# Block sums of the weights in smaller pieces over both halves of two batches, VectorE's part as scalar_tensor_tensor, the last token products three units sooner

## The chip, the cores and the metric

The kernel runs on one core of one Trainium2 chip. The metric is device microseconds of one execution (lower is better). The engines are named as in the profile: PE is TensorE (PEld its weight loads), DVE is VectorE, ACT is ScalarE, POOL is GpSimd, SP is SyncE, which here issues nearly all DMAs. Each engine takes its instructions in the order in which they were written for it.

## The reference

Attention with a local window and 24 block summaries per head, and then a mixer over tokens and over channels, for 4 batches of 768 tokens and 8 heads of 64:

```
k_sum, v_sum = max and mean of k, v over blocks of 32 tokens
scores = [local (|i-j| < 16) , q k_sum + log 32] / 8 ;  x = softmax(scores) @ [v, v_sum]
u  = x + (relu(x^T w_tok1) w_tok2)^T        # w_tok1 768x256, w_tok2 256x768
out = u + relu(u w_ch1) w_ch2               # w_ch1 512x1536, w_ch2 1536x512
```

## The kernel before

Matrix products run in a reduced fp32 form (fp32r): each operand is split into a high part (a copy on ACT) and the rest (a subtraction on DVE or POOL), and three of the four part products are summed. The work is written into a list by hand; a planner (`Plan._order`) with a cost and a rank for each item simulates the engines and fixes the order of the instructions of each engine. A lower rank goes first; the block sums have the last one (`R_BACK`).

Per batch b = 0..2 the channel mixer runs in 24 units called slots: 12 for the first 512 tokens (half 0) and 12 for the last 256 (half 1). In each, `ch1` multiplies u by one of 12 column blocks of w_ch1 (tile `hp`), ACT and DVE make the two parts of relu (tile `h`), and `ch2` adds h times a block of w_ch2 to the sums (`acc`); `ch1` of the next slot is written ahead of `ch2` of this one. Beside these slots stands the attention of batch b+1 (scores `sc`, products with v `av` that give `x`), and near their end the token products of batch b+1: `tok1x` makes high and low parts of x (`xs`) and of w_tok1 (`ws`), the low parts on POOL, 12 for a batch, and sums products into `t1q`; `tok2` multiplies its relu `t` by w_tok2 into `up` and makes `u`. `finish` adds u to `acc` on DVE and POOL (`ot`) and stores it.

Batch 3 goes another way: `last_mix` replaces eight block products of 2x2 blocks by seven (in two rounds, w_ch1 and w_ch2). It needs sums and differences of u's blocks (`t_2`, `t_3`, `t1`, `t4`, shown as `t`, from the scratch tiles `t32` and `t33`) and, for each of 6 row pairs k of both weights, four sums of weight blocks (s1 to s4). These twelve sets are made ahead by `weight_sums(w, k, tag)`: subtractions on POOL and DVE into `sz`, the high part on ACT into `sh`, the rest on POOL in place, then two DMAs of 512 KB to DRAM (`sums`), from which `last_mix` loads them. In the kernel before, each of batches 0 to 2 makes four sets, in slots 13, 14, 15 and 17, in buffers of the tags `u0` and `h`, which other tiles use too (`u0` holds u, `xs` and `ws`).

Of the kernel before, what the change touches and what calls it, by code (L numbers as in the profile page):

```python
# [189 lines left out]
def tile_attention_mixer(  # L190
# [574 lines left out]
    def tok2(b, half, p):  # L765
# [37 lines left out]
        if far:  # L803
# [9 lines left out]
            if whole and half and p < 2:  # L813
# [9 lines left out]
                lambda: (nc.vector, nc.gpsimd)[half].tensor_tensor(  # L823
                    out=u.t[:, 1], in0=xT(), in1=u.t[:, 0].bitcast(F32), op=ALU.subtract
                ),
# [144 lines left out]

    def weight_sums(w, k, tag):

        blk, keys = blocks(w, k)
# [6 lines left out]
        def step(eng, s, left, right, op):  # L980
            e = nc.gpsimd if eng == "pool" else nc.vector
            add(
                eng, 0.8 if eng == "pool" else 0.34,
                lambda: e.tensor_tensor(out=z.t[:, s], in0=left(), in1=right(), op=op),  # L984
                reads=keys, writes=[(z, s)], rank=R_BACK, behind=gate,
            )
# [17 lines left out]
        step("dve", 3, part("12", 0), own(1), ALU.subtract)
        step("dve", 3, own(3), part("12", 1), ALU.add)
        for ss in ((0, 1), (2, 3)):
            cs = slice(ss[0], ss[1] + 1)
# [5 lines left out]
            add(
                "pool", 1.1,
                lambda cs=cs: nc.gpsimd.tensor_tensor(  # L1015
                    out=z.t[:, cs].bitcast(F32R), in0=z.t[:, cs], in1=hi.t[:, cs].bitcast(F32),
                    op=ALU.subtract,
                ),
                reads=[(hi, ss)], writes=[(z, s) for s in ss], rank=R_BACK,
            )  # L1020
        add(
            "sp", 0.06, lambda: nc.sync.dma_start(out=away.t[:, 0], in_=hi.t.bitcast(F32)),
            reads=[(hi, ss) for ss in ((0, 1), (2, 3))], writes=[(away, 0)], kb=524,
        )
        add(
            "sp", 0.06, lambda: nc.sync.dma_start(out=away.t[:, 1], in_=z.t),
            reads=[(z, s) for s in range(4)], writes=[(away, 1)], kb=524,
        )
# [617 lines left out]
```

## Time and profile before

| | |
|---|---|
| median of 3 runs | 603.72 us (603.57 to 606.78) |
| the profiled execution | 604.11 us, its span 602.3 us |
| busy | PE 568.4, PEld 495.3, DVE 383.0, ACT 257.2, POOL 265.5 us |
| L984, subtractions of the sums | 60 on POOL; 60 on DVE, 50.0 us |
| L1015, low parts of the sums, POOL | 24, 32.8 us |
| L732, low parts of xs and ws, POOL | 36, 47.0 us |

The span is 1.8 us shorter than the execution's own time. Busy PE time counts overlapping matmuls to their modelled ends, so a stretch with no idle time may still run slower than PE could; the start of one group of matmuls to the start of the next is the better measure. In the rows, `x12` is a count of instructions, "[1.09 <-DVE h L870]" is idle time before the group and what ended it, and L984 is a line of the kernel. A helper's line stands for all its callers.

### The profile page before, as it was taken

How to read it: one execution, taken by the hardware profiler on the slowest of the kernel's cores; microseconds unless marked ns; L12 is line 12 of the kernel's file. 1: busy time of each engine (PE TensorE's matmuls, PEld its weight loads, DVE VectorE, ACT ScalarE, POOL GpSimd, SP SyncE). 2: the span in 40 equal slices, each digit the busy share in tenths (PEclk: the TensorE clock that was granted, in tenths of full speed). 3: DMA queues.
4: the chain of work that ended last, by engine and by line, in shares of the span. 5: the costliest groups of instructions: out<-in, count | busy, mean ns of one | idle time of the engine just before them, and what ended most of it. 6: DMA issues, size and time to landing. Idle time of an engine off the chain costs nothing. (4 is left out here: it accounts for less than half of the span.)

```text
span 602.3 us, 12729 instructions
## 1 busy us (share of the span) xinstructions
PE 568.4 (94%) x4629; PEld 495.3 (82%) x4629; DVE 383.0 (64%) x994; ACT 257.2 (43%) x777; POOL 265.5 (44%) x301
## 2 busy tenths in 40 slices
PE   8799999899889999999999799999998987999997
PEld 4588888778779978777889777877788976999997
DVE  4678799988993355354596255444369348435875
ACT  5577665444574342232242334242222433334542
POOL 0226586736872700000387850010059895344611
PEclk9889999999999999999999899999999998999999
DMA  8933568644776149687797654675485524578732
GB/s 276 344 115 124 187 222 264 210 140 162 257 233 209 52 141 261 177 269 196 230 233 268 172 102 133 138 186 144 97 205 159 171 104 140 194 234 266 245 106 75
DMA packets 139919, 112.12 MB, mean 186 GB/s; under 512 B 88272, under 2 KB 118608, under 8 KB 139856
## 3 DMA queue, kind: packets, MB, share of 16 engines
q1 hardware_dynamic: 139712, 111.10, 61.2%
q8 instruction: 37, 0.61, 0.4%
q14 instruction: 26, 0.21, 0.1%
q10 hardware_dynamic: 144, 0.20, 0.1%
HBM read 74.90 MB, written 34.60 MB: 182 GB/s over the span
## 5 line engine op out<-in xcount | busy, mean ns | idle before, releaser
L896 PE MATMUL acc<-h,w 128*128 128x512 f32 (+1 forms) x864 | 167.0, 342 | 4.5 <-DVE h L870 4.4
L853 PE MATMUL hp<-u,w 128*128 128x512 f32 (+1 forms) x864 | 165.5, 341 | 0.8 <-ACT u L817 0.6
L896 PEld LDWEIGHTS acc<-h,w 128*128 128x128 f32 x864 | 134.1, 189 | 25.8 <-DVE h L870 5.6
L853 PEld LDWEIGHTS hp<-u,w 128*128 128x128 f32 x864 | 134.2, 190 | 21.8 <-issue 1.3
L450 ACT ACTIVATE e<-e,den 128x120 f32<-128x120 f32 x192 | 73.3, 385 | 41.3 <-DVE den L440 35.1
L865 ACT ACTIVATE h<-hp 128x512 fp32r<-128x512 f32 (+1 forms) x72 | 35.1, 487 | 130.6 <-PE hp L853 130.4
L870 DVE SCALAR_TENSOR_TENSOR h<-hp,h 128x512 fp32r<-128x512 f32 (+1 forms) x72 | 39.6, 549 | 66.0 <-ACT h L865 66.0
L409 POOL MEMSET e<- 128x48 f32 x16 | 2.2, 138 | 129.8 <-DMA away<-e 74.3
L440 DVE CUSTOM_DVE_ANT_0 e<-sc,mask_sb 128x120 f32<-128x120 f32 x192 | 41.4, 276 | 10.9 <-PE sc L426 7.6
L790 PE MATMUL up<-wt,t 128*128 128x512 f32 (+2 forms) x192 | 42.3, 360 | 4.3 <-DVE t L685 2.7
L1460 POOL TENSOR_TENSOR w<-wb,w 128x256 fp32r<-128x256 f32 x48 | 38.0, 810 | 18.1 <-ACT w L1454 17.7
L790 PEld LDWEIGHTS up<-wt,t 128*128 128x128 f32 x192 | 32.2, 199 | 9.2 <-DVE t L685 4.4
L984 POOL TENSOR_TENSOR sz<-sz,w 128x256 f32<-128x256 f32 x48 | 37.9, 790 | 3.3
L1015 POOL TENSOR_TENSOR sz<-sz,sh 128x512 fp32r<-128x512 f32 x24 | 32.8, 1373 | 9.5 <-ACT sh L1010 4.7
L746 PE MATMUL t1q<-xs,ws 128*128 128x256 f32 x216 | 32.3, 302 | 4.7 <-POOL ws L732 3.2
L450 ACT ACTIVATION_READ_ACCUMULATOR e<-e,den 128x1 f32 x192 | 36.3, 189 | 0.0
L746 PEld LDWEIGHTS t1q<-xs,ws 128*128 128x128 f32 x216 | 29.8, 205 | 6.4 <-POOL ws L732 4.1
L984 DVE TENSOR_TENSOR sz<-sz,w 128x256 f32<-128x256 f32 x36 | 32.5, 908 | 0.8
L935 POOL TENSOR_TENSOR ot<-ot,u 128x512 f32<-128x512 f32 (+1 forms) x24 | 24.3, 1043 | 19.1 <-DVE ot L927 15.4
L426 PE MATMUL sc<-k,q 64*64 64x120 f32 x768 | 29.0, 275 | 1.9 <-PE et L488 0.7
L426 PEld LDWEIGHTS sc<-k,q 64*64 64x64 f32 x768 | 21.1, 135 | 10.8 <-issue 6.6
L557 PEld LDWEIGHTS av<-v,eT 120*64 120x64 f32 x768 | 24.0, 138 | 7.0 <-issue 4.7
(130 smaller groups left out, 899.4 us busy)
## 6 DMA issues: line engine op xcount, KB each, us to landing
w<-in_w_ch SPq DMA_DIRECT2D x48, 256.0 KB
k<-in_kw SPq DMA_DIRECT2D x16, 720.0 KB
v<-in_vw SPq DMA_DIRECT2D x32, 288.0 KB
q<-in_q SPq DMA_DIRECT2D x16, 384.0 KB
sums<-sh SPq DMA_DIRECT2D x12, 512.0 KB
...
```

Of the source, the lines that this page charges most:

```text
L426: nc.tensor.matmul(tiles[j].t[c * QT : (c + 1) * QT, i * NC : (i + 1) * NC], lhsT=qt.t[rows, t * QT : (t + 1) * QT], rhs=kt.t[rows, t, :], ...
L440: nc.vector.tensor_tensor_reduce(out=e.t[:, j, i * P : i * P + NC], in0=tiles[j].t[:, i * NC : (i + 1) * NC], in1=mask_sb[:, mv, :], op0=A ...
L450: nc.scalar.activation(ei, ei, AF.Exp, bias=den_t[n].t[:, 1, T : T + 1], scale=-1.0, accum_out=den_t[n].t[:, 0, T : T + 1],)
L746: nc.tensor.matmul(pt.t[:, 2 * P * k : 2 * P * (k + 1)], lhsT=ws[:, wp, T, ks], rhs=xs[:, xp, T], start=(c == 0 and k == 0 and T == 0 and ...
L790: nc.tensor.matmul(pt.t[:, :nt], lhsT=t1.t[:, part, ks], rhs=wt2[w].t[:, k, h0 : h0 + nt], start=(far and k == 0 and i == 0), stop=(k == D ...
L853: nc.tensor.matmul(pt.t[:, :nt], lhsT=w1_t[f].t[:, w, c], rhs=us[c].t[:, part], start=(i == 0), stop=(i == len(ops) - 1),)
L865: lambda: nc.scalar.activation(h.t[:, 0], pt.t[:, :nt], AF.Relu),
L870: lambda: nc.vector.scalar_tensor_tensor(out=h.t[:, 1], in0=pt.t[:, :nt], scalar=0.0, in1=h.t[:, 0].bitcast(F32), op0=ALU.max, op1=ALU.sub ...
L896: nc.tensor.matmul(slot.t[:, c0 : c0 + nt], lhsT=w2_t[f].t[:, w, o * P : (o + 1) * P], rhs=h.t[:, part], start=(f == 0 and w == 0 and part ...
L984: lambda: e.tensor_tensor(out=z.t[:, s], in0=left(), in1=right(), op=op),
L1015: lambda cs=cs: nc.gpsimd.tensor_tensor(out=z.t[:, cs].bitcast(F32R), in0=z.t[:, cs], in1=hi.t[:, cs].bitcast(F32), op=ALU.subtract,),
L1460: lambda hi=hi, lo=lo, source=source: nc.gpsimd.tensor_tensor(out=lo(), in0=source(), in1=hi().bitcast(F32), op=ALU.subtract),
```

## The change

`weight_sums` makes each set in two pieces. Piece 0 (s1, s2) is summed by POOL alone, 5 instructions; piece 1 (s3, s4) by DVE alone, 6 (5 before, since s4 now takes the two parts of piece 0's second sum in turn). Each piece has its own ACT copy, its own POOL remainder and two DMAs of 256 KB instead of a share of two DMAs of 512 KB. DVE's instructions there, in `last_mix`'s sums and splits, and in one split of `tok2` become `scalar_tensor_tensor` with a multiplication by 1 (`between`); the reciprocal's addition of 1e-9 becomes one too. The sets now stand in slots 14 and 17 of batch 0, and in 6, 8, 10, 13, 15 of batch 1 and 6, 8, 10, 12, 14 of batch 2; those of half 0 use the tag `t1`, the others `h`, none `u0`. For batch 3 the attention ends earlier (a1 is 26, not 29), `tok1x` stands in slots 16 and 17 (not 18 and 20), and `tok2` from slot 18 to 21 (not 20 to 22).

```diff
+    def between(eng, out_, left, right, op):
+        if eng == "pool":
+            nc.gpsimd.tensor_tensor(out=out_, in0=left, in1=right, op=op)
+        else:
+            nc.vector.scalar_tensor_tensor(
+                out=out_, in0=left, scalar=1.0, in1=right, op0=ALU.mult, op1=op
+            )
...
-                nc.vector.tensor_scalar(
-                    out=rec.t, in0=den.t[:, 0], scalar1=1e-9, scalar2=None, op0=ALU.add
+                nc.vector.scalar_tensor_tensor(
+                    out=rec.t, in0=den.t[:, 0], scalar=1e-9, in1=den.t[:, 0], op0=ALU.add,
+                    op1=ALU.max,
...
-        step("dve", 2, part("11", 0), part("21", 0), ALU.subtract)
-        step("dve", 2, own(2), part("11", 1), ALU.add)
-        step("dve", 2, own(2), part("21", 1), ALU.subtract)
...
-        step("dve", 3, part("12", 0), own(1), ALU.subtract)
-        step("dve", 3, own(3), part("12", 1), ALU.add)
...
+                step("dve", 0, part("11", 0), part("21", 0), ALU.subtract)
+                step("dve", 0, own(0), part("11", 1), ALU.add)
+                step("dve", 0, own(0), part("21", 1), ALU.subtract)
+                step("dve", 1, part("12", 0), old(1, 0), ALU.subtract)
+                step("dve", 1, own(1), old(1, 1), ALU.subtract)
+                step("dve", 1, own(1), part("12", 1), ALU.add)
...
-            for at_slot, tag in ((13, "u0"), (14, "h"), (15, "u0"), (17, "h")):
+    SUMS = ((14, 17), (6, 8, 10, 13, 15), (6, 8, 10, 12, 14))
+            if slot in SUMS[b]:
+                weight_sums(1 + n // HALF, n % HALF, "t1" if half == 0 else "h")
+        if b == B - 2:
+            a1 = 26
+            t1s = (16, 17)
-            t2s = [(20, 0, 0), (20, 0, 1), (21, 1, 0), (21, 1, 1)]
-            t2s += [(22, 1, 2), (22, 1, 3), (22, 0, 2), (22, 0, 3)]
+            t2s = [(18, 0, 0), (18, 0, 1), (19, 1, 0), (19, 1, 1)]
+            t2s += [(20, 1, 2), (20, 1, 3), (21, 0, 2), (21, 0, 3)]
```

How the engines' orders change, at three places. The first is PE at the end of batch 2's slots. `acc` ends these slots, `t1q` and `up` are batch 3's token products, `pa`, `pb`, `pc` are `last_mix`'s first products. Before:

```order
L896 MATMUL acc_1_0_5406<-h_1_10_5819,w_10_1630 128x256 x6
L896 MATMUL acc_1_2_5407<-h_1_10_5819,w_10_1630 128x256 x6
L896 MATMUL acc_1_0_5406<-h_1_11_5859,w_11_1719 128x256 x6
L896 MATMUL acc_1_2_5407<-h_1_11_5859,w_11_1719 128x256 x6
L746 MATMUL t1q_0_5775<-xs_0_1_5839,ws_0_1_5842 128x256 x12
L746 MATMUL t1q_0_5775<-xs_0_2_5856,ws_0_2_5861 128x256 x12
L790 MATMUL up_0_0_5922<-wt_0_632,t_3_0_5913 128x384
```

The same place of PE now:

```order
L895 MATMUL acc_1_0_5488<-h_1_10_6086,w_10_1630 128x256 x6
L895 MATMUL acc_1_2_5489<-h_1_10_6086,w_10_1630 128x256 x6
L895 MATMUL acc_1_0_5488<-h_1_11_6114,w_11_1719 128x256 x6
L895 MATMUL acc_1_2_5489<-h_1_11_6114,w_11_1719 128x256 x6
L1115 MATMUL pa_6134<-u_0_0_5801,w_0_885 128x384 x3
L1115 MATMUL pa_6134<-u_0_1_5816,w_0_885 128x384 x3
L1115 MATMUL pb_6146<-t_5942,s_0_5872 128x384 x6
L1115 MATMUL pc_6182<-t_6144,s_0_5955 128x384 x6
```

The five sets of `t1q` and eight `up` that stood behind the last `acc` (two sets and the first line of one `up` are shown) now all stand ahead of it, between slots 14 and 19 of 24, and `last_mix` follows `acc` at once. POOL at the same end: `ot` is batch 2's last sums, `t_6051` (now `t_6131`) is `t33`, `t_6067` (now `t_6144`) the low part of `t_3`, which `pc` reads, `t_0` and `t_1` are those of t4. Before:

```order
L935 TENSOR_TENSOR ot_1_0_5947<-ot_1_0_5947,u_1_3_4923 128x256
L1053 TENSOR_TENSOR t_6051<-u_1_1_5593,u_1_0_5321 128x384
L823 TENSOR_TENSOR u_1_2_6049<-u_1_1_5593,u_1_2_6049 128x384
L1068 TENSOR_TENSOR t_6067<-t_6051,t_6067 128x384
L1053 TENSOR_TENSOR t_6051<-u_1_1_5593,u_1_0_5321 128x384
L823 TENSOR_TENSOR u_1_3_6089<-u_1_1_5593,u_1_3_6089 128x384
L1068 TENSOR_TENSOR t_6067<-t_6051,t_6067 128x384
L1068 TENSOR_TENSOR t_0_6112<-t_6051,t_0_6112 128x384
```

POOL there now:

```order
L1040 TENSOR_TENSOR s_5_1_5891<-s_5_1_5891 128x512
L973 TENSOR_TENSOR t_6131<-u_1_1_5687,u_1_0_5400 128x384
L934 TENSOR_TENSOR ot_1_0_6129<-ot_1_0_6129,u_1_0_4651 128x256
L934 TENSOR_TENSOR ot_1_0_6129<-ot_1_0_6129,u_1_1_4761 128x256
L934 TENSOR_TENSOR ot_1_0_6129<-ot_1_0_6129,u_1_2_4910 128x256
L934 TENSOR_TENSOR ot_1_0_6129<-ot_1_0_6129,u_1_3_4915 128x256
L973 TENSOR_TENSOR t_6144<-t_6131,t_6144 128x384
L973 TENSOR_TENSOR t_6131<-u_1_1_5687,u_1_0_5400 128x384
L973 TENSOR_TENSOR t_0_6177<-t_6131,t_0_6177 128x384
L973 TENSOR_TENSOR t_6144<-t_6131,t_6144 128x384
```

The four `ot` stand between the first `t33` and its low part, so all of `t_3` now waits for `finish` of batch 2.

The second place is POOL at the end of batch 1's slots, ahead of batch 2's token products (`sz`, now `s`, are the sums; L1015, now L1040, their low parts). Before:

```order
L1015 TENSOR_TENSOR sz_0_3997<-sz_0_3997,sh_0_4090 128x512 x2
L732 TENSOR_TENSOR xs_0_0_4164<-x_0_3220,xs_0_0_4164 128x512
L732 TENSOR_TENSOR ws_0_0_4179<-wt_388,ws_0_0_4179 128x512
L984 TENSOR_TENSOR sz_1_4211<-w_1_1016,w_7_1464 128x256
L984 TENSOR_TENSOR sz_1_4211<-sz_1_4211,w_1_1016 128x256
L984 TENSOR_TENSOR sz_1_4211<-sz_1_4211,w_7_1464 128x256
L984 TENSOR_TENSOR sz_1_4211<-sz_1_4211,w_1_1016 128x256 x2
L1015 TENSOR_TENSOR sz_1_4211<-sz_1_4211,sh_1_4280 128x512 x2
L732 TENSOR_TENSOR xs_0_1_4315<-x_0_3220,xs_0_1_4315 128x512
```

POOL there now, where xs and ws 0_0 and 0_1 stand still further ahead:

```order
L733 TENSOR_TENSOR xs_0_2_4139<-x_0_3188,xs_0_2_4139 128x512
L733 TENSOR_TENSOR ws_0_2_4148<-wt_388,ws_0_2_4148 128x512
L1040 TENSOR_TENSOR s_5_1_4001<-s_5_1_4001 128x512
L973 TENSOR_TENSOR s_0_0_4143<-s_0_0_4143,w_0_929 128x256
L973 TENSOR_TENSOR s_0_0_4143<-s_0_0_4143,w_6_1383 128x256
L973 TENSOR_TENSOR s_0_0_4143<-s_0_0_4143,w_0_929 128x256 x2
L1040 TENSOR_TENSOR s_0_0_4143<-s_0_0_4143 128x512
L934 TENSOR_TENSOR ot_1_0_4322<-ot_1_0_4322,u_1_0_3010 128x256
L934 TENSOR_TENSOR ot_1_0_4322<-ot_1_0_4322,u_1_1_3141 128x256
L934 TENSOR_TENSOR ot_1_0_4322<-ot_1_0_4322,u_1_2_3252 128x256
L934 TENSOR_TENSOR ot_1_0_4322<-ot_1_0_4322,u_1_3_3341 128x256
L1040 TENSOR_TENSOR s_0_1_4308<-s_0_1_4308 128x512
```

The six instructions for the first half of x are now done ahead of the sums; behind the last row shown follow the six for the second half (xs_1, ws_1).

The third place is DVE in half 0 of batch 2, slots 8 and 9 (`h_0_8`, `h_0_9`; `rec` is the reciprocal of the attention's sums). Before:

```order
L870 SCALAR_TENSOR_TENSOR h_0_8_5129<-hp_0_8_5084,h_0_8_5129 128x512
L563 TENSOR_SCALAR rec_5137<-den_4980 128x6
L566 RECIPROCAL rec_5137<-rec_5137 128x6
L870 SCALAR_TENSOR_TENSOR h_0_9_5171<-hp_0_9_5142,h_0_9_5171 128x512
L870 SCALAR_TENSOR_TENSOR h_0_10_5204<-hp_0_10_5177,h_0_10_5204 128x512
```

DVE there now:

```order
L869 SCALAR_TENSOR_TENSOR h_0_8_5175<-hp_0_8_5132,h_0_8_5175 128x512
L975 SCALAR_TENSOR_TENSOR sl_2_1_5199<-w_2_1138 128x256
L975 SCALAR_TENSOR_TENSOR sl_2_1_5199<-sl_2_1_5199,w_2_1138 128x256 x2
L975 SCALAR_TENSOR_TENSOR sl_2_1_5199<-w_8_1528,sh_2_0_5180 128x256
L869 SCALAR_TENSOR_TENSOR h_0_9_5216<-hp_0_9_5185,h_0_9_5216 128x512
L975 SCALAR_TENSOR_TENSOR sl_2_1_5199<-sl_2_1_5199,sl_2_0_5145 128x256
```

Four instructions of a set of sums now stand between two `h`, where two short ones of the attention stood.

More of the change, by code (lines that the diff above doesn't have):

```diff
@@ L822, in tok2 @@
                 eng, took,
-                lambda: (nc.vector, nc.gpsimd)[half].tensor_tensor(
-                    out=u.t[:, 1], in0=xT(), in1=u.t[:, 0].bitcast(F32), op=ALU.subtract
-                ),
+                lambda: between(eng, u.t[:, 1], xT(), u.t[:, 0].bitcast(F32), ALU.subtract),
                 reads=[*parts, (u, 0)], writes=[(u, 1)], rank=R_EVAC,
@@ L1001, in weight_sums, with pair @@
-        step("pool", 1, own(0), part("11", 0), ALU.subtract)
-        step("pool", 1, own(1), part("11", 1), ALU.subtract)
-        keys = keys + [(z, 1)]
-        step("dve", 3, part("12", 0), own(1), ALU.subtract)
-        step("dve", 3, own(3), part("12", 1), ALU.add)
-        for ss in ((0, 1), (2, 3)):
-            cs = slice(ss[0], ss[1] + 1)
+        one = {}
+        def part(name, i):
+            return (lambda: blk[name](i)), keys
+        def pair(n):
+            if tag == "t1":
+                lo, hi = (
+                    sbuf([P, 2, 256], tag, f"s{x}_{w}_{k}_{n}", 4) for x in "lh"
+                )
+                views = [lambda: lo.t, lambda: hi.t]
+                slots = (lo, "lo"), (hi, "hi")
+            else:
+                slot = sbuf([P, 2, 2, 256], tag, f"s_{w}_{k}_{n}", 2)
+                views = [lambda: slot.t[:, 0], lambda: slot.t[:, 1]]
+                slots = (slot, "lo"), (slot, "hi")
+            return views, [[(s, (x, i)) for i in range(2)] for s, x in slots]
@@ new lines, in weight_sums, with own, old, step @@
+        for n in range(2):
+            (lo, hi), (lkeys, hkeys) = pair(n)
+            one[n] = lo, hi, lkeys, hkeys
+            def own(i, lo=lo, lkeys=lkeys):
+                return (lambda: lo()[:, i]), [lkeys[i]]
+            def old(i, x):
+                lo0, hi0, lk0, hk0 = one[0]
+                return ((lambda: lo0()[:, i]), [lk0[i]]) if x else ((lambda: hi0()[:, i]), [hk0[i]])
+            def step(eng, i, left, right, op, lo=lo, lkeys=lkeys):
+                add(
+                    eng, 0.78 if eng == "pool" else 0.36,
+                    lambda: between(eng, lo()[:, i], left[0](), right[0](), op),
+                    reads=left[1] + right[1], writes=[lkeys[i]], rank=R_BACK, behind=gate,
+                )
+            if n == 0:
+                step("pool", 0, part("21", 0), part("22", 0), ALU.add)
+                step("pool", 0, own(0), part("21", 1), ALU.add)
+                step("pool", 0, own(0), part("22", 1), ALU.add)
+                step("pool", 1, own(0), part("11", 0), ALU.subtract)
+                step("pool", 1, own(1), part("11", 1), ALU.subtract)
+            else:
+                step("dve", 0, part("11", 0), part("21", 0), ALU.subtract)
[4 more added lines that the diff above has]
+                step("dve", 1, own(1), part("12", 1), ALU.add)
@@ L1018, in weight_sums @@
+                reads=lkeys, writes=hkeys, rank=R_BACK,
+            )
+            add(
+                "pool", 1.3,
+                lambda lo=lo, hi=hi: nc.gpsimd.tensor_tensor(
+                    out=lo().bitcast(F32R), in0=lo(), in1=hi(), op=ALU.subtract
                 ),
-                reads=[(hi, ss)], writes=[(z, s) for s in ss], rank=R_BACK,
+                reads=hkeys, writes=lkeys, rank=R_BACK,
             )
[L1021 to L1028, printed above, removed]
+            for i, (view, vkeys) in enumerate(((hi, hkeys), (lo, lkeys))):
+                add(
+                    "sp", 0.06,
+                    lambda i=i, n=n, view=view: nc.sync.dma_start(
+                        out=away.t[:, i, 2 * n : 2 * n + 2], in_=view()
+                    ),
+                    reads=vkeys, writes=[(away, (n, i))], kb=262,
+                )
@@ L1046, in pe, with both @@
             )
-        def both(eng, out_, left, right, op, rank, extra=(), took=None):
-            e = {"pool": nc.gpsimd, "dve": nc.vector}[eng]
+        def both(eng, out_, left, right, op, rank):
             (o, oi), (l, li), (r, ri) = out_, left, right
             add(
-                eng, took or (0.85 if eng == "pool" else 0.48),
-                lambda: e.tensor_tensor(
-                    out=o.t[:, oi], in0=l.t[:, li], in1=r.t[:, ri], op=op
-                ),
-                reads=[left, right, *extra], writes=[out_], rank=rank,
+                eng, 1.05 if eng == "pool" else 0.5,
+                lambda: between(eng, o.t[:, oi], l.t[:, li], r.t[:, ri], op),
+                reads=[left, right], writes=[out_], rank=rank,
             )
```

43 lines of the change are left out of this document (9 added, 34 removed).

## The prediction

> **What bounds the kernel now.** I read the page first. The share of busy time names PE.
>
> ```profile
> PE 568.4 (94%) x4629; PEld 495.3 (82%) x4629; DVE 383.0 (64%) x994; ACT 257.2 (43%) x777; POOL 265.5 (44%) x301
> ```
>
> The change takes no product from PE, so all it can give is time that PE waits. I cut the span into stages, in us of the span; columns are busy time of PE, PEld, DVE, ACT, POOL (count), then PE's granted clock, DMA share and GB/s.
>
> ```profile
> 140.00:190.00 50.00, 44.20 (x569) 41.19 (x568) 44.28 (x133) 27.45 (x101) 34.35 (x36) 0.97 0.72 238
> 190.00:300.00 110.00, 109.96 (x803) 91.33 (x801) 51.07 (x171) 36.32 (x123) 20.35 (x24) 1.00 0.62 180
> 300.00:365.00 65.00, 58.28 (x510) 52.82 (x509) 39.07 (x80) 21.87 (x51) 46.60 (x49) 0.95 0.67 186
> 365.00:450.00 85.00, 85.00 (x666) 68.55 (x665) 42.78 (x156) 28.35 (x114) 9.86 (x15) 1.00 0.62 154
> 450.00:512.00 62.00, 53.75 (x424) 51.12 (x423) 40.16 (x61) 22.41 (x47) 52.83 (x51) 0.97 0.48 147
> ```
>
> PE stands still in three stages, the ends of batches 0, 1 and 2, where all sums are made; in the two stages between, PE has no idle time and POOL almost no work. The same cut for the sums' line alone (DVE, POOL):
>
> ```profile
> 140.00:190.00 50.00, 17.36 (x20) 15.92 (x20) 0.97 0.72 238
> 300.00:365.00 65.00, 14.96 (x20) 15.77 (x20) 0.95 0.67 186
> 450.00:512.00 62.00, 14.71 (x18) 15.20 (x20) 0.97 0.48 147
> ```
>
> In the first stage DVE is busy for 44.3 of 50 us, 17.4 of them for the sums. PE's waits there, and one group in which the clock was halved:
>
> ```profile
> PE et L488 <- DVE x L569: 3.9, 3, 1.4
> PE av L557 <- issue: 1.6, 1, 1.6
> ```
>
> ```profile
> 178.58 2.91 PE L853 MATMUL hp<-u,w 128*128 128x256 f32 x12
> ```
>
> The price of PE work comes from a dense place:
>
> ```profile
> 327.18 1.54 PE L853 MATMUL hp<-u,w 128*128 128x256 f32 x12
> 328.56 1.58 PE L896 MATMUL acc<-h,w 128*128 128x256 f32 x12
> ```
>
> From start to start 12 matmuls of 256 columns take 1.38 us, say 1.4; by columns 12 of 512 take 2.8 and 6 of 384 take 1.05 (estimates from these rows). With this the lost time of a stage can be counted where the idle column hides it.
>
> **Term A, end of batch 0: -5.0.** Lost: 3.9 + 1.6 of waits and 2.91 - 1.54 = 1.4 in the halved clock, 6.9 us. Two sets of sums leave this stage. DVE had 20 instructions of 17.36/20 = 0.87 us; now 12, at the same 0.87, 10.4 us. DVE's load falls from 44.3 to 37.3 of 50, and POOL's by half its sums. I take 5.0: the waits fall on `x`, queued on DVE behind the sums, and two sets still stand there. Bounds: 0 (the waits fall where those two are) and 6.9.
>
> Whether scalar_tensor_tensor is cheaper than tensor_tensor decides that 0.87. The rows (min, median, max in ns) of the sums, and of the kernel's own two-SBUF-input scalar_tensor_tensor, whose wt rows ran before POOL had work and whose wb rows ran beside it:
>
> ```profile
> L984 DVE TENSOR_TENSOR sz<-sz,w x36: 382/852/1529, 145.9 to 478.5; 128x256 f32<-128x256 f32 x36
> L1431 DVE SCALAR_TENSOR_TENSOR wb<-w,wb x17: 409/691/1196, 40.8 to 129.6; 128x512 int32<-128x512 int32 x9, 128x256 int32<-128x256 int32 x8
> L1431 DVE SCALAR_TENSOR_TENSOR wt<-w,wt x3: 691/691/692, 25.1 to 29.6; 128x512 int32<-128x512 int32 x3
> ```
>
> Undisturbed, 256 columns take 0.38 to 0.41 us in both forms; beside POOL both stretch, to 1.53 and 1.20. So the form costs or brings nothing: 0, with bounds of -0.46 us for each instruction of the sums (never held) and +0.27 (below). The 32 short reciprocal sums go with it. The Trainium skill speaks against the form: "Vector Engine (DVE) Microarchitecture Reference", section "Points that are easy to get wrong", says that scalar_tensor_tensor with two SBUF sources that are not bf16 runs at half throughput. The wt rows, 512 columns of two SBUF sources in 0.69 us, disagree; by the rule they would be some 1.2 us.
>
> **Term B, end of batch 1: -3.5.** PE between the last `av` and the next batch's second score:
>
> ```profile
> 334.33 1.62 PE L557 MATMUL av<-v,eT 120*64 120x64 f32 x48
> 335.88 1.69 PE L896 MATMUL acc<-h,w 128*128 128x256 f32 x12
> ...
> 351.67 3.03 PE L746 MATMUL t1q<-xs,ws 128*128 128x256 f32 x24
> ...
> 363.38 0.85 PE L426 MATMUL sc<-k,q 64*64 64x120 f32 x24
> ```
>
> From the end of `acc` (335.88 + 1.4 = 337.3) to 363.38 are 26.1 us, for five sets of `t1q` (7.0), four `up` of 6x512 (5.6) and one `hp` of 12x512 (2.8): 15.4. Lost 10.7. Two waits of `acc` for `h` behind sums, 1.09 here and 1.71 in batch 2, are of the same kind:
>
> ```profile
> 314.38 1.46 PE L896 MATMUL acc<-h,w 128*128 128x256 f32 x10 [1.09 <-DVE h L870]
> ```
>
> ```profile
> 464.20 1.46 PE L896 MATMUL acc<-h,w 128*128 128x256 f32 x10 [1.71 <-DVE h L870]
> ```
>
> POOL's prices, from batch 3's token products before:
>
> ```profile
> 485.04 1.29 POOL L1015 TENSOR_TENSOR sz<-sz,sh 128x512 fp32r<-128x512 f32 x1
> ...
> 491.31 0.75 POOL L935 TENSOR_TENSOR ot<-ot,u 128x256 f32<-128x256 f32 x1
> 492.01 1.31 POOL L732 TENSOR_TENSOR xs<-x,xs 128x512 fp32r<-128x512 f32 x1
> 493.27 1.31 POOL L732 TENSOR_TENSOR ws<-wt,ws 128x512 fp32r<-128x512 f32 x1
> 494.53 2.11 POOL L935 TENSOR_TENSOR ot<-ot,u 128x256 f32<-128x256 f32 x3
> 501.05 1.39 POOL L1053 TENSOR_TENSOR t<-u,u 128x384 f32<-128x384 f32 x1 [4.41 <-DVE u L807]
> 502.40 1.01 POOL L823 TENSOR_TENSOR u<-u,u 128x384 fp32r<-128x384 f32 x1
> ```
>
> Now the first three sets of `t1q` are ready early. After E, the end of the last `acc`, POOL still has four `ot` (to E+2.7), one low part of sums (1.3, E+4.0) and three pairs of xs and ws of 2.5 us: E+6.5, E+9.0, E+11.5. PE does `av` and two `up` meanwhile and then follows POOL; its last `t1q` ends at E+13. From there it is as before, 351.67 + 2.8 = 354.5 to 363.38, 8.9 us. E+21.9, with work of 1.6 + 5.6 + 4.2 + 2.8 = 14.2: lost 7.7. The gain is 10.7 - 7.7 = 3.0, and 1.1 for `h`; I take 3.5. Bounds: 0 (the low part of sums is late by the 4 us, since it waits for DVE) and 8 (xs and ws cause no wait, 3.3 stay).
>
> **Term C, end of batch 2: -3.3.** PE from the second `t1q` to the first `pc`:
>
> ```profile
> 482.40 1.92 PE L746 MATMUL t1q<-xs,ws 128*128 128x256 f32 x14
> ...
> 506.69 1.30 PE L1095 MATMUL pa<-u,w 128*128 128x384 f32 x6 [0.95 <-DVE u L807]
> 507.84 0.87 PE L1095 MATMUL pb<-t,s 128*128 128x384 f32 x4
> 510.07 0.62 PE L1095 MATMUL pb<-t,s 128*128 128x384 f32 x2 [1.36 <-DVE t L1068]
> 510.52 1.23 PE L1095 MATMUL pc<-t,s 128*128 128x384 f32 x6
> ```
>
> 28.1 us for five sets of `t1q` (7.0), eight `up` of 6x384 (8.4), `pa` and `pb` (2.1), 17.5: lost 10.6, and 1.7 for `h`. Now token products stand among slots: POOL's 10 xs and ws after the first pair (13), one 512-wide `ot`, five sums and one low part make some 20 us, beside about 21 us of PE work over the same stretch; I leave 1.5 us of waits. The new wait comes at the end. With F the end of the last `acc`, DVE's part of `ot` lets POOL begin at about F, four `ot` end at F+2.9, and then come, in order, `t_3`'s first low part (1.3), the second `t33` (1.4), t4's first (1.3) and `t_3`'s second (1.3): F+8.2. PE is through `pa` and `pb` at F+2.1 and waits for `pc` 6.1 us; such a hole halves the clock, 1.4 as above. Lost 1.5 + 6.1 + 1.4 = 9.0 against 12.3. Bounds: +2 (POOL falls behind PE among the slots as well) and -9 (`pc`'s wait and the clock's vanish, since ends are modelled late).
>
> Queued behind these POOL waits are `ot`'s stores on SP and loads for k=1, which PE needs at F+7 at the earliest, so they hide behind `pc`'s wait; without it they have 5 us.
>
> **Term D, half 0 of batches 1 and 2: +1.5.** Six sets move where PE never waited. SP gets 48 DMAs of 256 KB instead of 24 of 512, the same bytes; in the stages between, the DMA share was 0.62, so they fit, though SP's queue waits behind each for POOL. DVE has room (51 of 110 us, 43 of 85), but `h` stands behind the sums:
>
> ```profile
> L865 ACT ACTIVATE h<-hp 128x512 fp32r<-128x512 f32 x36 | 21.3, 593 | 74.0 <-PE hp L853 73.9
> L870 DVE SCALAR_TENSOR_TENSOR h<-hp,h 128x512 fp32r<-128x512 f32 x36 | 24.6, 683 | 39.2 <-ACT h L865 39.2
> ```
>
> PE covers `h` with one `hp`, 2.8 us; ACT and DVE need 0.59 + 0.68, so 1.5 us are to spare. Four sums in a row take 3.5 us at 0.87 and are 1.9 late if `h` comes due just as they begin. Of some 12 such groups I let less than one hit in full: 1.5. Bounds 0 and 23 (all twelve).
>
> **The sum.** -5.0 - 3.5 - 3.3 + 1.5 = -10.3. The profiled execution took 604.11 us (span 602.3), 0.39 over the median: 593.8 by it, 593.4 by the median; I say 593.5.
>
> **The rivals.**
> - *Given back at the ends.* B's low part and C's waits take their upper bounds, A holds: -5 + 0 + 2 would be 600.7; with half of it, 599. For it: POOL's order around `ot` is plain; against: it needs two places.
> - *Sums ahead of `h`, slower.* A, B and C bring 11.8, so D has to pass 14.8 for a loss of over 0.5% (3 us, about what a measurement of this kernel can tell from no change): eight of the twelve groups in full, 15.2. With ten, 19.0, it gives 611. Against it: in the trace only two such waits of `acc`, 1.09 and 1.71, came of sums beside `h` in half 1, with less cover.
> - *scalar_tensor_tensor is not held by POOL.* Then 0.87 falls to 0.41: A takes all of 6.9, D nothing, B 4.1 with its sums on time, C 4: 588.6. Against it: the wb row's 1196 ns.
> - *Half rate.* 0.27 more per sum: A's DVE relief falls from 7.0 to 3.8 and A to 2.7, D's groups grow by 1.1 to some 3: about 597.5. Against it: the wt row. It is the skill's rule of term A.
> - *No change.* The waits only change their names: 603.
>
> **How the numbers follow.** My forecast, 589.5 to 597.5: 0.50. Given back, 597.5 to 600.7: 0.18. Not held, under 589.5: 0.12. Half rate: 0.04. No change within 3 us: 0.08. Slower: 0.08. Faster is 0.50 + 0.18 + 0.12 + 0.04 = 0.84. The range leaves out the slow cases, and most of "no change": 586 (A, B and C near the bounds) to 601.5.
>
> **What the profile after would show.** A: no waits of `et` for `x` between 140 and 190, and DVE under 40 us there. B: PE's `t1q` waits for ws three times in a row after the last `av`. C: one wait of `pc` for POOL's `t`, 4 to 7 us, right after `pa` and `pb`, and none of `up`. D: PE idle for `h` in the stages that had none. The form: L975's median on DVE near 0.85 us. I am wrong if the hole before `pc` is missing, if half 0 loses more than 5 us, or if L975 runs at 0.41 beside POOL.

## The result: half of the forecast gain, and where the rest stayed

The changed kernel takes 599.04 us (median of 10 runs, 596.19 to 601.08), the kernel before 603.64 beside it (10 runs, 601.83 to 606.78). The ratio is 0.9917, its 95% interval 0.989 to 0.9944: 5.0 us faster, 3.4 to 6.6. The forecast was 10.3 us, 593.5. The profiled execution took 600.40 us (span 598.6), 3.7 less than that of before.

The page's busy times of the changed kernel, and the same cut into stages as in the prediction (PE, PEld, DVE, ACT, POOL, then PE's granted clock, DMA share, GB/s):

```profile
PE 567.8 (95%) x4629; PEld 495.2 (83%) x4629; DVE 371.2 (62%) x1006; ACT 257.0 (43%) x777; POOL 260.8 (44%) x301
```

```profile
140.00:190.00 50.00, 47.97 (x619) 45.08 (x612) 35.59 (x135) 29.36 (x107) 26.99 (x28) 1.00 0.65 205
190.00:300.00 110.00, 110.00 (x808) 91.99 (x808) 58.35 (x171) 36.14 (x116) 37.54 (x43) 1.00 0.69 207
300.00:365.00 65.00, 56.03 (x490) 49.03 (x492) 31.99 (x96) 21.98 (x67) 27.86 (x33) 0.95 0.58 150
365.00:450.00 85.00, 84.10 (x663) 68.25 (x656) 49.84 (x160) 30.58 (x111) 29.45 (x37) 1.00 0.72 188
450.00:512.00 62.00, 55.60 (x432) 53.76 (x431) 33.37 (x57) 20.12 (x44) 38.51 (x37) 0.94 0.46 131
```

POOL's work did move: 46.6 to 27.9 us at the end of batch 1, and 20 to 38 in half 0 before it, where PE still has no idle time. Yet PE's busy time at the end of batch 1 fell, from 58.3 to 56.0 of 65, where it should have risen. The idle column misses half-clock time, so I counted lost time as in the prediction: for each matmul, start to start above the fast quarter of its shape.

| stage, us | lost before | lost after | difference | forecast |
|---|---|---|---|---|
| 0 to 120 (start) | 33.2 | 34.5 | +1.3 | none |
| 120 to 190, A | 20.3 | 14.5 | -5.8 | -5.0 |
| 190 to 300 and 370 to 450, D | 20.0 | 20.4 | +0.4 | +1.5 |
| 300 to 370, B | 18.1 | 20.6 | +2.5 | -3.5 |
| 450 to 515, C | 14.7 | 12.4 | -2.3 | -3.3 |
| 515 to the end | 2.5 | 2.5 | 0 | none |

The sum is -3.9, the profiled spans differ by -3.7. The start holds nothing of the change but the reciprocals; over all the kernels below it loses 31.5 to 34.5 us, so single executions differ by some 3 us there alone. In this pair of traces three terms came out within 1.1 us of their size, and B has the wrong sign and is off by 6.0 us, more than all that is missing. The experiments' traces, counted in the same way, say how firm that is: e1, e2, e3 and e6 leave the end of batch 1 as it is in the changed kernel and lose 20.5 to 21.8 us there, so B's loss is no scatter. For C it is otherwise: e1, e3, e5 and e10, which have the changed kernel's end of batch 2, lose 11.0 to 14.1 us there, and e9, which has that of before, 13.5, so a gain of 2.3 is hardly more than scatter.

PE's waits in the changed kernel, the longest first:

```profile
PE t1q L747 <- POOL ws L733: 3.4, 4, 1.0
PE pc L1115 <- POOL t L973: 2.3, 2, 1.3
...
PE hp L852 <- DVE u L975: 1.5, 2, 1.3
PE up L791 <- DVE t L686: 1.4, 1, 1.4
...
PE et L488 <- DVE x L570: 1.0, 1, 1.0
```

Three of the four waits for `ws`, 0.81 to 0.84 us each, are what B foretold (the fourth, 1.0, stands elsewhere); `pc`'s are C's. Those of `up` and `hp` for DVE are the new ones. PE at the end of batch 1:

```profile
331.63 0.57 PE L557 MATMUL av<-v,eT 120*64 120x64 f32 x12
...
344.68 1.46 PE L747 MATMUL t1q<-xs,ws 128*128 128x256 f32 x10 [0.81 <-POOL ws L733]
...
348.79 3.77 PE L791 MATMUL up<-wt,t 128*128 128x512 f32 x10 [1.44 <-DVE t L686]
...
355.17 1.58 PE L852 MATMUL hp<-u,w 128*128 128x512 f32 x5 [1.30 <-DVE u L975]
...
360.09 4.60 PE L852 MATMUL hp<-u,w 128*128 128x512 f32 x12
```

The last `t1q` ends at 346.1, 14.5 us after the last `acc` (forecast 13; POOL begins its `ot` 1.4 us after that `acc`, when DVE's half of them is there, and the forecast let it begin at once). Then the next batch's scores, at 359.31, come 13.2 us later, where before it was 8.9, and 12 matmuls of 512 columns, 3.06 us at the full clock (e5), took 4.60. What `up` and `hp` wait for stands on DVE, and DVE itself waits for DMAs: the additions of `up` to `xT`, one for each of four pairs of heads (called heads here; the first and the last addition are shown), and SP, which issues them (start, time on SP, tile, count):

```profile
347.71 0.69 DVE L808 TENSOR_TENSOR xT<-up,xT 128x512 f32<-128x512 f32 x1 [6.44 <-DMA xT<-xaway]
...
356.52 0.69 DVE L808 TENSOR_TENSOR xT<-up,xT 128x512 f32<-128x512 f32 x1 [0.57 <-DMA xT<-xaway]
```

```profile
331.49 5.16 SPq L530 DMA_DIRECT2D xT<-xaway  x8
336.75 0.55 SPq L1048 DMA_DIRECT2D sums<-s  x1
337.40 1.37 SPq L945 DMA_DIRECT2D out<-ot  x3
...
340.73 0.57 SPq L530 DMA_DIRECT2D xT<-xaway  x1
...
343.86 1.17 SPq L644 DMA_DIRECT2D xaway<-xb  x2
...
347.73 6.67 SPq L530 DMA_DIRECT2D xT<-xaway  x10
```

```profile
L530 SPq DMA_DIRECT2D xT<-xaway x32: 557/614/1323, 331.5 to 385.7; - x32
```

The last fence gives min, median and max in ns of these reads. All four additions wait for a DMA last (6.44, 1.06, 1.91 and 0.57 us). x goes to DRAM (`xaway`) and is read back transposed (`xT`) in 16 reads of 64 KB for half 0; each holds SP for some 0.6 us, and SP, which runs in order, issues with hardly a pause from 331.5 to 354.4. First come eight reads for the other half (`xT` of heads 0 and 1, not needed until slot 2 of the next batch), then a store of sums and the stores of `ot`; the store of the last head's `xaway`, whose x was ready at 336.4, goes out at 343.9. Before, `ot` was added up later, its stores stood behind all but the last four reads, and the store of `xaway` waited 3.5 us:

```profile
341.22 1.09 SPq L643 DMA_DIRECT2D xaway<-xb  x2
...
354.74 1.05 SPq L946 DMA_DIRECT2D out<-ot  x2
```

The Trainium skill says where to look for this: "Perfetto Trace Analysis", section "Optimizing DMA Performance", calls a kernel bound by the DMA sequencer when the issuing engine's track is solid DMA slices. SP's rows here agree, at a DMA share of 0.55 between 330 and 370 us. But the sign alone does not decide it, since in the kernel before SP is as solid at this place (334.5 to 359.6); that it was the bound is what e3, e5, e9 and e10 test.

### The profile page after: what moved, and what is told of

The parts are those of the page before. It is cut to its first block, busy times and chain, and to the rows that moved or that the text cites. A ratio compares the mean times of both kernels' runs of the same rounds, so it can differ in the third digit from the quotient of the medians.

```text
span 598.6 us, 12794 instructions
## 1 busy us (share of the span) xinstructions
PE 567.8 (95%) x4629; PEld 495.2 (83%) x4629; DVE 371.2 (62%) x1006; ACT 257.0 (43%) x777; POOL 260.8 (44%) x301
## 4 chain that ended last, share of the span: by engine, by line
PE 64%; DVE 11%; DMA 8%; POOL 6%; issue 3%; SPq 3%; ACT 3%; DVEq 0%; POOLq 0%; ACTq 0%
PE acc L895 17%; PE hp L852 17%; PE sc L426 3%; PE av L557 3%; PE pb L1115 3%; PE qb L1115 3%; DMA w<-in_w_ch 3%; PE qa L1115 2%; PE t1q L747 2%; PE pc L1115 2%; PE pa L1115 2%; PE qc L1115 2%; PE up L791 2%; POOL ot L934 2%; DVE wb L1451 1%
## 5 line engine op out<-in xcount | busy, mean ns | idle before, releaser
L791 PE MATMUL up<-wt,t 128*128 128x512 f32 (+2 forms) x192 | 40.4, 353 | 1.9 <-DVE t L686 1.4
L934 POOL TENSOR_TENSOR ot<-ot,u 128x512 f32<-128x512 f32 (+1 forms) x24 | 23.8, 1020 | 29.0 <-DVE ot L926 29.0
L1040 POOL TENSOR_TENSOR sl<-sl,sh 128x512 fp32r<-128x512 f32 x12 | 15.5, 1289 | 44.0 <-ACT sh L1035 44.0
L747 PE MATMUL t1q<-xs,ws 128*128 128x256 f32 x216 | 29.4, 285 | 4.0 <-POOL ws L733 3.4
L747 PEld LDWEIGHTS t1q<-xs,ws 128*128 128x128 f32 x216 | 27.2, 190 | 5.4 <-POOL ws L733 4.2
L557 PE MATMUL av<-v,eT 120*64 120x64 f32 x768 | 26.6, 224 | 4.2 <-DMA eT<-away 2.2
L426 PEld LDWEIGHTS sc<-k,q 64*64 64x64 f32 x768 | 20.9, 135 | 10.4 <-issue 5.9
L570 DVE TENSOR_TENSOR x<-av,rec 128x384 f32<-128x384 f32 x32 | 17.4, 552 | 18.7 <-PE av L557 17.6
L1474 ACT ACTIVATE w<-wb 128x256 fp32r<-128x256 f32 x48 | 18.1, 413 | 23.8 <-DVE wb L1451 23.7
```

Of the source, the lines that this page charges most:

```text
L426: nc.tensor.matmul(tiles[j].t[c * QT : (c + 1) * QT, i * NC : (i + 1) * NC], lhsT=qt.t[rows, t * QT : (t + 1) * QT], rhs=kt.t[rows, t, :], ...
L557: nc.tensor.matmul(pv[cs, T], lhsT=eT[:NC, T % (TT // 2), cs], rhs=v.t[:NC, 2 * T + c], start=True, stop=True,)
L747: nc.tensor.matmul(pt.t[:, 2 * P * k : 2 * P * (k + 1)], lhsT=ws[:, wp, T, ks], rhs=xs[:, xp, T], start=(c == 0 and k == 0 and T == 0 and ...
L791: nc.tensor.matmul(pt.t[:, :nt], lhsT=t1.t[:, part, ks], rhs=wt2[w].t[:, k, h0 : h0 + nt], start=(far and k == 0 and i == 0), stop=(k == D ...
L934: lambda view=view, u=u: nc.gpsimd.tensor_tensor(out=view(), in0=view(), in1=u.t[:, 1].bitcast(F32), op=ALU.add),
```

## The experiments

Each was timed in five rounds beside the kernel before on the same chip. The ratio to before is the figure to compare; 0.0033 of it is 2 us.

### e1: the form alone

```
-            nc.vector.scalar_tensor_tensor(
-                out=out_, in0=left, scalar=1.0, in1=right, op0=ALU.mult, op1=op
-            )
+            nc.vector.tensor_tensor(out=out_, in0=left, in1=right, op=op)
```

> Only the form is undone: every two-input VectorE operation of between() is tensor_tensor again (sums, the low parts of the token products and of the last products); the reciprocal's scalar_tensor_tensor stays. Theory (the form is neutral, what got shorter is the sums that no longer run beside GpSimd): within 1.5 us of the changed kernel, so 597.5 to 600.5, and the sums of batch 0's end still near 0.5 us each. Rival (scalar_tensor_tensor is what made the sums shorter): sums back at 0.85 us and 2 us or more slower. Rival (half rate): faster by about 0.27 us for each of the 36 sums that are in PE's way, 2 us or more.

Measured: 599.41 us, ratio 0.9931 (0.9904 to 0.9958), against 0.9917: no difference that can be told. One group of the sums, min/median/max in ns, of the changed kernel and then of e1:

```profile
L975 DVE SCALAR_TENSOR_TENSOR s<-s,w x18: 381/426/1418, 153.0 to 486.9; 128x256 f32<-128x256 f32 x18
```

```profile
L975 DVE TENSOR_TENSOR s<-s,w x18: 411/425/1412, 149.6 to 485.4; 128x256 f32<-128x256 f32 x18
```

Both take 0.42 us alone and up to 1.4 when a POOL operation runs beside them. Of DVE's 72 sums, 51 ran with no POOL operation beside them, in e1 as in the changed kernel; before the change 8 of 60. There is no half rate here (0.69 for 256 columns would be it, an estimate from the 0.69 that 512 columns took). So the rule of the Trainium skill that the prediction weighed ("Vector Engine (DVE) Microarchitecture Reference", section "Points that are easy to get wrong") does not hold for these fp32 operands.

### e2: the last token products where they were

```
-            a1 = 26
-            t1s = (16, 17)
+            a1 = 29
+            t1s = (18, 20)
```

and t2s and the fetches two slots later, as before the change.

> The last batch's attention and token products stand where they stood before (a1 29, t1s 18 and 20, t2s 20 to 22, fetches in 18 and 19), all else as in the changed kernel. Theory (the move is worth what the stage 450 to 512 shows, 14.8 us lost before and 12.5 after): 2 to 3 us slower than the changed kernel, 601 to 602. Rival (the hole before pc takes all that the move brings): within 1 us. Rival (without the move GpSimd is late with xs and ws behind new sums as well): over 4 us slower.

Measured: 598.24 us, ratio 0.9911 (0.9883 to 0.994). The move is worth nothing that can be told; the first rival. The hole before `pc` is there as well (1.33, 1.72 and 1.18 us), and of before's waits of `t1q` and `up` one of 0.8 us is left, without the move: between 450 and 515 it loses 13.8 us, the changed kernel 12.4, before 14.7.

### e3: the reads for the other half behind

```
-        fetch(xa_t.pop((b, half, p)), slot, lambda: slot.t, HT[b][half] // 5)
+        w = fetch(
+            xa_t.pop((b, half, p)), slot, lambda: slot.t, HT[b][half] // 5,
+            behind=state["far"] if half else (),
+        )
+        if not half:
+            state["far"] = [w]
```

`w` is the last of a head's four reads; what is `behind` it is issued after it.

> At the end of batch 1 the eight transposed reads of xT for the other half of heads 0 and 1 (32 KB, 0.62 us of SP's queue each, not needed until slot 2 of the next batch) wait behind the sixteen that the next batch's first hp needs. Nothing else is changed. Theory (the end of batch 1 is bound by SP's queue: from 331.5 to 354.4 us it issues without a pause, and PE's up and hp wait for the xT that come last): 8 x 0.62 = 5.0 us less ahead of the last xT, of which PE gets 3 to 5 and one stretch at half clock, 1.4, goes: 593 to 596. Rival (GpSimd's xs and ws set the end, as the prediction had it): PE's t1q ends at 346 in both, at most 1 us, 598 to 599. Rival (the xT wait for buffers of the tag e, not for the queue): no change.

Measured: 598.12 us, ratio 0.9913 (0.9882 to 0.9945), no gain against the changed kernel's 0.9917. My number failed. SP in e3, in the place of the eight reads:

```profile
332.26 0.33 SPq L1055 DMA_DIRECT2D sums<-s  x1
332.80 1.71 SPq L952 DMA_DIRECT2D out<-ot  x3
...
336.46 0.57 SPq L530 DMA_DIRECT2D xT<-xaway  x1
...
348.61 1.77 SPq L295 DMA_DIRECT2D v<-vs  x2
350.47 7.91 SPq L530 DMA_DIRECT2D xT<-xaway  x12
```

The eight reads had stood in time that SP in part spends waiting anyway, for the sums' copy on ACT and for `ot` on POOL, ahead of `xT` in the queue: the first `xT` goes out 6.3 us after the first `av`, in the changed kernel 9.1, so 2.8 us are won and not 5.0. These are lost again further on: the two stores of `xaway` hold SP for 2.9 us instead of 1.2, and the reads of the last head stand behind two DMAs `v<-vs`, which in the changed kernel come after them; they begin 20.3 us after the first `av`, there 20.2. From the first `av` to the scores it is 27.7 us, as in the changed kernel. So either the queue is not the bound, or what else stands in it holds it as well as the eight reads: e5.

### e4: the sums in half 1 only

```
-    SUMS = ((14, 17), (6, 8, 10, 13, 15), (6, 8, 10, 12, 14))
+    SUMS = ((13, 14, 15, 17),) * 3
```

> The sums stand in slots 13, 14, 15 and 17 of each batch, as before the change, in their new smaller pieces; the rest as in the changed kernel. Theory (the gain at the end of batch 0, 5.8 us by the lost time of 120 to 190, comes from sums that left this stage): it goes, and 3 to 6 us slower than the changed kernel, 602 to 605. Rival (the smaller pieces make the gain, since VectorE's no longer run beside GpSimd's): within 2 us of the changed kernel.

Measured: 606.92 us, ratio 1.0064 (1.0033 to 1.0096): 3.9 us slower than before and 8.9 slower than the changed kernel, worse than expected. Where the sums stand decides the time, and with all of them in half 1 the gain is gone. But not as I expected: batch 0's end keeps its gain (13.8 lost), since part of its sums run over into the next stage, which loses 16.6 instead of 9.5, and `pc` waits 11.4 us at the end of batch 2, where POOL, with sums until 505.4 us, comes to `t` only then and after `ot`. The end of batch 1 is better than in the changed kernel, with 12.9 us lost from 300 to 370 instead of 20.6: there `t1q` and `up` stand among the last slots and no longer behind them. Which of the moved sums does this was not tested. The long wait, and POOL's rows:

```profile
PE pc L1115 <- ACT t L1083: 11.4, 1, 11.4
```

```profile
505.40 2.77 POOL L934 TENSOR_TENSOR ot<-ot,u 128x256 f32<-128x256 f32 x4
508.12 1.96 POOL L973 TENSOR_TENSOR t<-u,u 128x384 f32<-128x384 f32 x2
```

### e5: the queue cleared

As e3, and for the stores of `ot` of batch 1's half 1 and of the last set's second pair of sums:

```
+        late = state["far"] if (b, h0) == (1, 512) else ()
...
-            reads=keys, kb=nt // 2,
+            reads=keys, kb=nt // 2, behind=late,
```

> As e3, and at the end of batch 1 the four stores out<-ot and the two stores of the last sums (slot 15, second pair) wait on SP behind the sixteen reads xT too; no engine's arithmetic changes. In e3 SP stood between the reads from 330.7 to 336.4, waiting for the sums' copy on ACT and for ot on GpSimd. Theory (SP runs in order, and what the change put ahead of xT is what holds it; the first xT then starts at about 332 instead of 336.5, its add at about 338, and head 3's xT, which needs the buffer of head 0's xT, can start at about 341): PE then follows GpSimd's xs and ws, up and hp run on from the last t1q at 345 to 351 instead of 358, 4 to 7 us and the half clock less: 591 to 594.5. Rival (the chain over the buffer, add of head 0, u, read of head 3, add, u, some 9 us from the first add, stays as long as it was): under 1.5 us, 596.5 to 598. Rival (the sixteen reads are slow in themselves): no change.

Measured: 591.39 us, ratio 0.9809 (0.9778 to 0.984): 11.5 us faster than before and 6.5 faster than the changed kernel, with the arithmetic of every engine unchanged. SP, DVE's first and third addition to `xT` (the second and fourth wait for nothing), and PE:

```profile
332.18 1.92 SPq L530 DMA_DIRECT2D xT<-xaway  x3
...
343.49 3.34 SPq L530 DMA_DIRECT2D xT<-xaway  x5
```

```profile
340.38 0.69 DVE L818 TENSOR_TENSOR xT<-up,xT 128x512 f32<-128x512 f32 x1 [2.39 <-DMA xT<-xaway]
...
347.19 0.69 DVE L818 TENSOR_TENSOR xT<-up,xT 128x512 f32<-128x512 f32 x1 [1.90 <-PE up L801]
```

```profile
344.22 4.58 PE L801 MATMUL up<-wt,t 128*128 128x512 f32 x12 [1.02 <-ACT t L691]
...
352.08 0.85 PE L426 MATMUL sc<-k,q 64*64 64x120 f32 x24
352.85 3.06 PE L862 MATMUL hp<-u,w 128*128 128x512 f32 x12
```

The first read starts at 332.2 (340.7 in the changed kernel), only the first addition waits for a DMA, the third for PE's own `up`, and after the scores `hp` runs at the full clock (3.06). From the first `av` to the scores it is 23.9 us instead of 27.7, and from the end of the last `t1q` to the scores 8.9, which is the figure that the prediction had carried over, instead of 13.2. Both hold in every trace: in the four kernels with the queue cleared (e5, e7, e8, e12) these stretches are 23.8 to 25.0 and 8.8 to 9.0 us, in the five without (the changed kernel, e1, e2, e3, e6) 27.7 to 30.0 and 12.8 to 15.5. That SP's queue held this end is shown. These 4 us are the part of the 6.5 that can be traced to this place; the rest is not traced. The stage now waits for POOL's `xs` and `ws`, as the prediction had it.

### e6: `ot` on DVE

```
-                "pool", spent(nt, 0.7, 1.2),
+                "dve" if (b, half) == (2, 1) else "pool", spent(nt, 0.7, 1.2),
```

> At the end of batch 2's second half the four second additions of ot are made by VectorE instead of GpSimd; nothing else differs from the changed kernel. Theory (the hole before pc, three waits of 1.33, 1.72 and 0.94 us for t, and the half clock behind it, 2 us, come from t's low part standing behind ot on GpSimd): the first wait goes and most of the second, 3 to 5 us, 594.5 to 596.5. Rival (t waits for the chain GpSimd difference, ACT copy, GpSimd or VectorE low part, whoever is first): one wait stays, 1 to 2 us, 597 to 598.5. Rival: VectorE's ot now delays hb, no gain.

Measured: 594.87 us, ratio 0.9852 (0.9816 to 0.9888): 3.9 us faster than the changed kernel. The first products of batch 3, in the changed kernel and then in e6:

```profile
501.53 0.62 PE L1115 MATMUL pc<-t,s 128*128 128x384 f32 x2 [1.33 <-POOL t L973]
503.88 0.69 PE L1115 MATMUL pc<-t,s 128*128 128x384 f32 x1 [1.72 <-ACT t L1083]
505.50 1.01 PE L1115 MATMUL pc<-t,s 128*128 128x384 f32 x2 [0.94 <-POOL t L973]
506.31 2.12 PE L1115 MATMUL pa<-u,w 128*128 128x384 f32 x6
```

```profile
499.76 0.62 PE L1117 MATMUL pc<-t,s 128*128 128x384 f32 x2 [0.32 <-POOL t L975]
500.22 1.22 PE L1117 MATMUL pa<-u,w 128*128 128x384 f32 x6
```

The waits fall from 4.0 to 0.3 us, and the half clock behind them (2.12 for six matmuls, twice, 1.22 in e6) goes. The hole and its cause, `t` behind `ot` on POOL, are shown.

### e7 and e8: both, and `ot` of batch 1 on DVE too

> e5 and e6 together. Theory: the two stages do not touch each other, so the gains add: 8 to 11 us off the changed kernel, 588 to 591. Rivals: as for e5 and e6, what one does not bring is missing here too.

> As e7, with batch 1's second ot additions on VectorE too, so GpSimd begins xs and ws at the end of batch 1 2.8 us sooner. Theory (with the queue cleared the end of batch 1 is bound by GpSimd's pairs of xs and ws, 2.5 us each, as the prediction had it): 2 to 2.8 us less than e7. Rival (xT through SP still comes last there): the same as e7 within 1 us.

Measured: e7 589.58 us, ratio 0.9776 (0.9744 to 0.9808), the fastest here with e8: 13.5 us faster than before, 8.5 than the changed kernel. By the ratios the two gains are 6.5 and 3.9, 10.4 together; the missing 1.9 is within the intervals. e8: 590.18, ratio 0.9776 (0.9738 to 0.9813), no more than e7, which is its rival's number. The rival's reason is there in part, as the last addition to `xT` waits 1.5 us for a DMA. But mainly the move gives POOL no earlier start. POOL begins its `xs` 6.0 us after the first `av`, no sooner than in e5 (5.5): `x`, of which they are made, now stands on DVE behind the additions to `ot`, and the first `up` waits for it too:

```profile
333.30 3.02 PE L801 MATMUL up<-wt,t 128*128 128x512 f32 x12 [1.45 <-DVE x L572]
```


### e9: the queue cleared in the kernel before

> The kernel before, with SP's queue cleared at the end of batch 1 as in e5: reads of xT for the next half, the last sums' low store and the stores of ot behind the sixteen reads. Theory (before the change GpSimd's xs and ws for the last three sets of t1q set this end, and the reads landed in their shadow; the queue became the bound only when the change took that GpSimd work away): within 1.5 us of before, 601 to 603.5. Rival (SP's queue was the bound before the change too): 4 us or more faster, 599 or less.

Measured: 602.4 us beside 604.1, ratio 0.9968 (0.994 to 0.9996), 1.9 us (0.2 to 3.6) faster, near the theory's 1.5; the interval ends short of the rival's 4. PE's chain there is still POOL's:

```profile
340.46 5.49 PE L756 MATMUL t1q<-xs,ws 128*128 128x256 f32 x24 [1.34 <-POOL ws L742]
```

So before the change POOL was the bound of this end, as the prediction read it, and the queue ran in its shadow.

### e10: only the stores behind

> As e5, but the eight reads for the other half stay where the changed kernel has them, ahead of the sixteen; only the stores of ot and of the last sums wait behind. e3 (reads moved, stores not) brought 1 us, e5 (both) 7.6. Theory (SP is short of issue time, so both must go: 8 x 0.62 of reads are back ahead of the sixteen, but they fall where SP waits for eT's buffers and the copy anyway): about half, 3 to 5 us, 594 to 596. Rival (the stores that wait for GpSimd are the whole of it): within 1.5 us of e5, 590 to 593. Rival (either alone brings nothing): 597 to 599.

Measured: 596.76 us beside 604.1, ratio 0.9903 (0.9865 to 0.9941): 0.8 us faster than the changed kernel by the ratios, less than the half that I expected and nearest the last rival. The eight reads hold SP from 329.8 to 335.0, and with it the loads `vb`, the last of which goes out at 339.3; what follows is a chain over three engines to PE:

```profile
343.50 0.29 POOL L390 TENSOR_SCALAR vs<-vs 96x128 f32<-96x128 f32 x1 [1.76 <-DVE vs L382]
343.88 1.28 POOL L743 TENSOR_TENSOR ws<-wt,ws 128x512 fp32r<-128x512 f32 x1
```

```profile
345.21 1.46 PE L757 MATMUL t1q<-xs,ws 128*128 128x256 f32 x10 [2.98 <-POOL ws L743]
```

DVE's sum of `vb` was late, POOL's `vs` waited for it with the last `ws` behind it, and PE waited 2.98 us (in the changed kernel `vs` stands behind the last `ws` on POOL; the planner puts it ahead in e5 too, where it costs half a microsecond). Behind this wait the stretch from the last `t1q` to the scores is 9.8 us, so the queue no longer holds `up` and `hp`; the eight reads cost their time through `vb` instead. With e3 and e5: by the ratios either alone brings less than 1 us, both bring 6.5. In e3 the rest of the queue fills most of the time that the reads leave; in e10 the reads hold back another load.

### e11: the sums moved in one piece

In the kernel before, the loop over slots 13, 14, 15 and 17 becomes:

```
+            if slot in ((14, 17), (6, 8, 10, 13, 15), (6, 8, 10, 12, 14))[b]:
+                n = len(sd)
+                weight_sums(1 + n // HALF, n % HALF, "u0" if half == 0 else "h")
```

> The kernel before, with the sums in the changed kernel's slots (14 and 17; 6, 8, 10, 13, 15; 6, 8, 10, 12, 14) but in one piece with stores of 512 KB, VectorE's part as tensor_tensor, and the token products where they were. Theory (where the sums stand is what makes the change's gain; pieces, form and token products bring nothing that can be measured): within 2 us of the changed kernel, 597 to 601. Rival (the smaller pieces are needed, since VectorE's and GpSimd's sums run beside each other again and their stores of 512 KB hold SP): no faster than before, 602 to 605.

Measured: 613.9 us, ratio 1.019 (1.0147 to 1.0234): neither, 11.5 us slower than before. The edit did not do what it says. The sums' line by stage (DVE, POOL):

```profile
240.00:300.00 60.00, 2.41 (x4) 5.53 (x8) 1.00 0.81 236
300.00:365.00 65.00, 13.92 (x22) 14.07 (x18) 0.92 0.62 171
```

Written into half 0, most of batch 1's sums still ran at its end, now five sets instead of four, and PE waited 8.0 us at a stretch for `ws` there; the end of batch 2 lost 8 us more than before as well (450 us to the end). I take it that they waited for buffers of `u0`, which `xs` and `ws` take later in the list; that is argued, not shown. Two things follow: the sums do not run in half 0 by being written there, and what lets them is the smaller pieces or the tag `t1` that these take, which no run separates; and A needs neither the pieces nor the form, since this kernel loses 15.0 us from 120 to 190, against 14.5 and 20.3.

### e12: e7 with the token products back

> e7 with the last token products where they stood before the change. Theory (the products' move brings nothing; e2 said so with the hole before pc still there): within 1.5 us of e7, 588 to 591. Rival (the hole hid what the move brings): 2 us or more slower than e7, 592 or more.

Measured: 589.88 us, ratio 0.9768 (0.9733 to 0.9804), the same as e7. The earlier token products bring nothing with the holes gone, either.

## Why the prediction was right or wrong

**Term A, right.** -5.8 against -5.0. Of three waits of `et` for `x`, 3.9 us, one of 1.0 is left (the sign said none), the clock of the stage is 1.00, DVE is busy for 35.6 us (under 40, as said). Every other kernel here with fewer sums at this end loses 13.4 to 15.1 us in this stage, so the gain is no scatter. The sums' 0.87 us was wrong in a way that did no harm: 12 took 6.47 us, 0.54 each.

```profile
140.00:190.00 50.00, 6.47 (x12) 1.00 0.65 205
```

**The form, the step right, the mark wrong.** "0" holds (e1), but the median near 0.85 that I gave as its sign came out at 0.42. I carried over a duration from sums that ran beside POOL's; now DVE's part reads POOL's results and comes after them, mostly alone. The 10 sums that still ran wholly beside a POOL operation have a median of 0.84 us, so scalar_tensor_tensor is held by POOL as tensor_tensor is (0.85 for 11 such sums in e1).

**Term B, wrong, and more than the whole of the miss.** +2.5 against -3.5, outside its bounds of -8 and 0. The first half of the step was near: the waits for `ws` come as written, and `t1q` ends at E+14.5 instead of E+13, since POOL's `ot` wait for DVE's first. The sentence that failed is "From there it is as before, 351.67 + 2.8 = 354.5 to 363.38, 8.9 us". It took 13.2, and `hp` behind it 1.5 us longer than at the full clock. I asked what on POOL and PE stood between, and not what the next steps read: `xT` comes through 16 reads on a queue that was solid in the trace of before too, and I counted queued stores in C, where they did no harm, and none in B, although I had put the additions to `ot` ahead of the token products on POOL, so that their stores come ahead of `xT` on SP. With the queue cleared the same stretch takes 8.8 to 9.0 us in four kernels, so the failed step was this one and the queue is its cause. e9 shows that the queue was not the bound before, so its cost could not be read off as a wait; it had to be counted as a chain. That does not make B right: with the queue cleared the stage from 300 to 370 loses 16.3 us in e5 and 16.4 to 18.8 in e7, e8 and e12, against 18.1 before, so B would have brought 1.8 us at most, and what took the rest is open beyond the 1.5 us at `t1q`. That e5's 591.4 us lie inside the likeliest case's range is thus not B's doing.

**Term C, the hole right, the size not shown, the cause wrong.** -2.3 against -3.3 in this pair of traces; with the others it is 11.0 to 14.1 us lost after against 13.5 and 14.7 before, so the gain may be anything from none to the whole forecast. The hole before `pc` is there, and behind `ot` on POOL (e6): three waits of 4.0 us in sum and 1.8 for the clock, against 6.1 and 1.4; one of the three is for ACT. But the earlier token products, to which I gave the gain, bring nothing: e2 and e12 put them back and lose nothing. What gain there is must then come from the sums that left the stage; that is argued, not tested by itself.

**Term D, right.** +0.4 against +1.5; PE has no wait for `h` in half 0, only one of 0.9 for `eT`. The sum over both halves hides no more than traces scatter (e1, e2, e3 and e6 lose 19.4 to 20.6 us there), so the lower bound, 0, was the better guess, since the sums take 0.47 and 0.54 us there, not 0.87:

```profile
190.00:300.00 110.00, 8.46 (x18) 1.00 0.69 207
...
365.00:450.00 85.00, 9.75 (x18) 1.00 0.72 188
```

**The rivals.** The time, 599.0, is the one that I gave for "given back at the ends" (599, chance 0.18), and it was given back at one of the two ends named. That is luck: the mechanism was another, not the low part of the sums on POOL, but SP's queue. And 599 does not follow from the prediction's own terms: halfway to their upper bounds B and C give -1.75 and -0.65, with A's -5.0 and D's +1.5 some 597.8; the 600.7 leaves out D as well.
